# Block ends of a fused scan and expert kernel: the sixth product's bank summed later, and a last step with an order of its own

## The chip, the cores and the metric

One core of one Trainium2 chip. The metric is device microseconds of one execution. A ratio is the mean time of one kernel's fast runs over that of the other's in the same rounds, so it isn't quite the ratio of the medians that are quoted with it. "Span" is what the profile shows, from the first to the last instruction; the time of an execution is about 1.8 us longer.

## The reference

A Mamba-2 scan in chunks gives the rows of `x`, and four experts work on every row, weighted by probabilities:

```python
# x, B, C: (4, 8, 768, 32 or 16); out: (3072, 256)
x = attn_out.transpose(0, 2, 1, 3).reshape(3072, 256)
p = domain_probs / (domain_probs.sum(-1, keepdims=True) + 1e-09)
for e in range(4):
    h = np.maximum(x @ w1[e], 0.0)
    out += p[:, e:e + 1] * (h @ w2[e])
```

## The kernel before

All is fp32. The rows are worked in six blocks of 512. A block has eight steps, one for each pair of expert and slice of its hidden width. In a step both matrix products are done in seven products instead of eight (a Strassen-like scheme): `fmul` gives the first layer into banks X and Y, VectorE sums and gates them (`total`, `gated`) and takes differences T1 to T4 (`diff`), and `smul` adds the second layer's products to four PSUM banks `acc0` to `acc3`, two products a bank. The products of step n - 1 are issued between those of step n, so a block's last products fall into the next block's first step. There `keep` copies two banks to SBUF, and `combine` adds the products up to the result.

```python
ORDER = (1, 3, 7, 5, 6, 2, 4)            # products, two a bank: 6 and 2 share acc2

def combine(k, part, eng):
    p1, p3 = kept[k, 0][:, 0], kept[k, 0][:, 1]
    # ... o, u: result and partial sums in SBUF; b1, b2: halves of the block
    if part == 0:
        nc.vector.tensor_add(u[:, 0], acc[k, 2][:, 0], p1)      # product 6's half of acc2
    if part == 1:
        p7, p5 = kept[k, 1][:, 0], kept[k, 1][:, 1]
        eng.tensor_add(u[:, 1], u[:, 0], p7)
        eng.tensor_add(u[:, 2], u[:, 0], p5)
        eng.tensor_add(o[:, 1, b2], u[:, 1], p5)
        eng.tensor_add(o[:, 0, b2], u[:, 2], p3)
    if part == 2:
        nc.vector.tensor_add(o[:, 0, b1], acc[k, 2][:, 1], p1)
        nc.vector.tensor_add(o[:, 1, b1], acc[k, 3][:, 0], u[:, 1])

def leave(k, lo, n, queues):             # 32x32 transposes on VectorE, then 8 transfers
    # ...
    nc.vector.transpose(ot.rearrange("p d b j -> p d (b j)"), o[:, :, lo:lo + n])
    for q in range(P // 32):
        for d in range(2):
            queues[d].dma_start(out=dst[q, d], in_=ot[32 * q:32 * q + 32, d])

for n in range(NS + 1):                  # the last turn only finishes step NS - 1
    # ... products 1, 3, 7, 5 of step n - 1 between those of step n
    smul(n - 1, 6)
    if ending:                           # first step of a block
        combine(k - 1, 0, nc.vector)
        combine(k - 1, 1, nc.gpsimd if run else nc.vector)
        if not run:
            leave(k - 1, HB, HB, (nc.sync, nc.scalar))
    if run:
        diff(n, "T3", "22", "12")
    smul(n - 1, 2)
    if c_in is not None:
        scores(...); masked(...)         # the scan of the next block
    smul(n - 1, 4)
    if run:
        diff(n, "T1", "12", "11"); diff(n, "T2", "22", "T1"); diff(n, "T4", "21", "T2")
    if ending:
        combine(k - 1, 2, nc.vector)
        if not run:
            leave(k - 1, 0, HB, (nc.sync, nc.scalar))
```

Of the kernel before, what the change touches and what calls it, by code (L numbers as in the profile page):

```python
# [8 lines left out]
FP32 = mybir.dt.float32  # L9
# [3 lines left out]
P = 128  # L13
# [4 lines left out]
def kernel(  # L18
# [32 lines left out]
    nc = tc.nc  # L51
# [60 lines left out]
    def load_w1(n):  # L112
        e, jj = divmod(n % SPB, JJ)
        t1 = wt1[n] = wts.tile([P, 7, HB], FP32, tag="wt1", name="wt1")
        if n >= SPB:
            nc.sync.dma_start(out=t1, in_=w1_d[n % SPB])
            return
        for k in range(2):
            nc.sync.dma_start(
                out=t1[:, 2 * k:2 * k + 2],  # L120
                in_=w1[e, k * P:k * P + P].rearrange("p (a f) -> p a f", a=2)[
                    :, :, jj * HB:jj * HB + HB])

    def load_w2(n):
        e, jj = divmod(n % SPB, JJ)
        t2 = wt2[n] = wts.tile([P, 7 * HB], FP32, tag="wt2", name="wt2", bufs=4)
        if n >= SPB:
            nc.sync.dma_start(out=t2, in_=w2_d[n % SPB])
            return
        for i in range(2):  # L130
            f = i * FH + jj * HB
            nc.sync.dma_start(
                out=t2[:, i * 2 * HB:(i + 1) * 2 * HB].rearrange("p (j m) -> p j m", j=JJ),
                in_=w2[e, f:f + HB].rearrange("(j p) m -> p j m", p=P))
# [88 lines left out]
    def load_gate(k, e):  # L223
        g = gate[k, e] = ffn.tile([P, CPB, P], FP32, tag="gate", name="gate", bufs=3)
        nc.sync.dma_start(out=g, in_=p_d[CPB * k:CPB * k + CPB, e].partition_broadcast(P))
# [112 lines left out]
    def sums(k):  # L338

        y = yT[k]  # L340
        b1, b2 = slice(0, HB), slice(HB, BLK)
        Y = yS[k] = ffn.tile([P, 4, HB], FP32, tag="yS", name="yS")
        nc.vector.tensor_sub(Y[:, 0], y[:, 0, b2], y[:, 0, b1])
        nc.vector.tensor_sub(Y[:, 1], y[:, 1, b2], Y[:, 0])
        nc.vector.tensor_sub(Y[:, 2], y[:, 1, b2], y[:, 0, b2])
        nc.vector.tensor_sub(Y[:, 3], y[:, 1, b1], Y[:, 1])
# [4 lines left out]
    def fmul(n, i):  # L351

        k = n // SPB
        f = first.setdefault(n, {})
        bank = "X" if i in (1, 6, 7, 4) else "Y"
        if i in (1, 2, 5):
            f[bank] = ps_f.tile([P, JJ, HB], FP32, tag=bank, name=bank)
        y, Y = yT[k], yS.get(k)
        w = (A11, A12, S4, A22, S1, S2, S3)[i - 1]
        b1, b2 = slice(0, HB), slice(HB, BLK)  # L360
        rhs = {1: y[:, 0, b1], 2: y[:, 1, b1], 3: y[:, 1, b2]}.get(i)
        if rhs is None:
            rhs = Y[:, {4: 3, 5: 0, 6: 1, 7: 2}[i]]
        for j in range(JJ):
            nc.tensor.matmul(  # L365
                out=f[bank][:, j], lhsT=wt1[n][:, w, j * P:j * P + P], rhs=rhs,
                start=(i in (1, 2, 5) and j == 0), stop=(j == JJ - 1), skip_group_check=True)

    def snap(n, i):

        s = first[n][i] = ffn.tile([P, JJ, HB], FP32, tag="snap", name="snap", bufs=4)
        nc.scalar.copy(out=s, in_=first[n]["X"])  # L372

    def total(n, i, b):

        z = first[n]["z" + b] = ffn.tile([P, JJ, HB], FP32, tag="z", name="z", bufs=3)
        nc.vector.tensor_add(z, first[n]["Y"], first[n][i])  # L377

    def gated(n, b, src):

        if n not in hid:
            hid[n] = {}
        h = hid[n][b] = ffn.tile([P, JJ, HB], FP32, tag="h" + b, name="h" + b)
        k, e = n // SPB, n % SPB // JJ
        half = int(b[1]) - 1
        g = gate[k, e].rearrange("p c s -> p (c s)")[:, half * HB:half * HB + HB]
        nc.vector.scalar_tensor_tensor(  # L387
            out=h, in0=first[n][src], scalar=0.0, in1=g.unsqueeze(1).to_broadcast([P, JJ, HB]),
            op0=ALU.max, op1=ALU.mult)

    def diff(n, o, x, y):
        h = hid[n]
        h[o] = ffn.tile([P, JJ, HB], FP32, tag="h" + o, name="h" + o)
        nc.vector.tensor_sub(h[o], h[x], h[y])  # L394
# [22 lines left out]
        e = kept[k, u] = ffn.tile([P, 2, HB], FP32, tag=f"kept{u}", name=f"kept{u}", bufs=1)  # L417
        nc.scalar.copy(out=e, in_=acc[k, u])

    def combine(k, part, eng):  # L420

        p1, p3 = kept[k, 0][:, 0], kept[k, 0][:, 1]
        if part == 0:
            kept[k, "o"] = ffn.tile([P, 2, BLK], FP32, tag="o", name="o", bufs=1)
            kept[k, "u"] = ffn.tile([P, 3, HB], FP32, tag="u", name="u", bufs=1)
        o, u = kept[k, "o"], kept[k, "u"]
        b1, b2 = slice(0, HB), slice(HB, BLK)
        if part == 0:
            nc.vector.tensor_add(u[:, 0], acc[k, 2][:, 0], p1)  # L429
        if part == 1:  # L430
            p7, p5 = kept[k, 1][:, 0], kept[k, 1][:, 1]
            eng.tensor_add(u[:, 1], u[:, 0], p7)
            eng.tensor_add(u[:, 2], u[:, 0], p5)
            eng.tensor_add(o[:, 1, b2], u[:, 1], p5)
            eng.tensor_add(o[:, 0, b2], u[:, 2], p3)
        if part == 2:
            nc.vector.tensor_add(o[:, 0, b1], acc[k, 2][:, 1], p1)
            nc.vector.tensor_add(o[:, 1, b1], acc[k, 3][:, 0], u[:, 1])

    def leave(k, lo, n, queues):  # L440

# [10 lines left out]
    def opened(n):  # L452

        fmul(n, 1)
        snap(n, 1)
        fmul(n, 2)
# [38 lines left out]


    both = nc.sync, nc.sync
    for n in range(NS + 1):
        k, r = divmod(n, SPB)

        enter, exit = ({1: 0, 2: 1, 4: 2, 6: 3}, {2: 0, 3: 1, 5: 2, 7: 3}) if k == 0 else (
            {0: 0, 2: 1, 4: 2, 6: 3}, {1: 0, 3: 1, 5: 2, 7: 3})
        c_in, c_out = (CPB * (k + 1) + d[r] if r in d and k < NBLK - 1 else None
                       for d in (enter, exit))
        ending = r == 0 and k > 0
        run = n < NS
        if run:
            e = r // JJ
            if r % JJ == 0 and n + JJ < NS:
                load_gate(*divmod(n // JJ + 1, E))  # L510
            if n + 2 < NS:
                load_w1(n + 2)
                load_w2(n + 2)
            if n:
                opened(n)
                total(n, 1, "11")
                gated(n, "11", "z11")
        if c_in is not None:
            masks(c_in)
            decays(c_in)  # L520
        if n + 2 < NS:
            sum_w1(n + 2)
            sum_w2(n + 2)
        if r == 1 and k > 0:
            leave(k - 1, 0, BLK, both)
        smul(n - 1, 1)
        if run:
            if n == 0:
                fmul(n, 5)
            fmul(n, 6)  # L530
            snap(n, 6)
        smul(n - 1, 3)
        if ending:
            keep(k - 1, 0)
        if c_out is not None:
            outputs(c_out, ps_att, "att")
            added(c_out, ps_att, "att")
        if run:
            if n:
                fmul(n, 5)  # L540
            fmul(n, 7)
            snap(n, 7)
            total(n, 7, "22")
        smul(n - 1, 7)
        smul(n - 1, 5)
        if ending:
            keep(k - 1, 1)
        if run:
            gated(n, "22", "z22")
        if c_out is not None:  # L550
            carry(c_out)
            if c_out + 2 < NCH:
                load_chunk(c_out + 2)
        if run:
            fmul(n, 3)
            total(n, 6, "12")
            fmul(n, 4)
            gated(n, "21", "X")
            gated(n, "12", "z12")
            if r == SPB - 1 and k < NBLK - 1:  # L560
                sums(k + 1)
        smul(n - 1, 6)
        if ending:
            combine(k - 1, 0, nc.vector)
            combine(k - 1, 1, nc.gpsimd if run else nc.vector)
            if not run:
                leave(k - 1, HB, HB, (nc.sync, nc.scalar))
        if run:
            diff(n, "T3", "22", "12")
        smul(n - 1, 2)  # L570
        if c_in is not None:
            scores(c_in, ((ps_att, "att"), (ps_att, "att"), (ps_f, "X"), (ps_f, "Y")))
            masked(c_in, (2, 3, 0, 1))
        smul(n - 1, 4)
        if run:
            diff(n, "T1", "12", "11")
            diff(n, "T2", "22", "T1")
            diff(n, "T4", "21", "T2")
        if ending:
            combine(k - 1, 2, nc.vector)  # L580
            if not run:
                leave(k - 1, 0, HB, (nc.sync, nc.scalar))


# [43 lines left out]
```

## Time and profile before

| | |
|---|---|
| time, median of the four executions compared with the change | 680.52 us (679.91 to 680.96) |
| span of the profiled execution | 677.0 us |
| TensorE busy, share of the chain that ended last | 95%, 89% |
| TensorE halts on u, inside the run and in the last step | 5 of 0.85 us, 1 of 0.59 us |
| one product, start to start | 0.865 us |

The prediction below shows the lines.

### The profile page before, as it was taken

Reading aid. Unit: us, or ns where it says so; the run is one execution under the profiler, and the core shown is the slowest. Engines: PE = TensorE matmul, PEld = TensorE weight load, DVE = VectorE, ACT = ScalarE, POOL = GpSimd, SP = SyncE. Lnnn points to the kernel's source line nnn. Section 1 sums busy time; section 2 is a strip of 40 time slices with the busy share of each in tenths; the row PEclk is TensorE's granted clock in tenths of the full one; section 3 lists DMA queues with packets and bytes.
Section 4 is the critical chain, followed back from the end, with each engine's and each line's share of the span. In section 5 each row is a group of like instructions: output and inputs, shape, how many; then the busy total and the mean of one; then the engine's idle time right before and its main releaser. Section 6 shows DMA issues by size and latency. Waiting matters only on the chain.

```text
span 677.0 us, 9047 instructions
## 1 busy us (share of the span) xinstructions
PE 643.3 (95%) x3465; PEld 538.6 (80%) x3465; DVE 504.7 (75%) x821; ACT 116.2 (17%) x231; POOL 107.9 (16%) x153
## 2 busy tenths in 40 slices
PE   3779999999999999999999999999999999999995
PEld 1458788888888887888887888887888888888884
DVE  6979887697776867876878768668868776856655
ACT  1111112121211121121112111212211112111110
POOL 2976845001000002000002000002000000200000
PEclk9989999999999999999999999999999999999999
DMA  8997859636745554765364655554673543653202
GB/s 247 337 326 251 293 194 345 245 120 183 253 160 182 189 201 129 243 234 180 121 231 153 205 188 193 196 179 163 186 258 127 180 161 109 171 218 119 99 1 31
DMA packets 70938, 128.64 MB, mean 190 GB/s; under 512 B 29040, under 2 KB 52464, under 8 KB 70896
## 3 DMA queue, kind: packets, MB, share of 16 engines
q1 hardware_dynamic: 65688, 112.67, 49.3%
q0 software_dynamic: 2304, 14.68, 5.7%
q10 hardware_dynamic: 2904, 0.72, 0.5%
q8 instruction: 27, 0.44, 0.3%
q14 instruction: 15, 0.12, 0.1%
HBM read 109.99 MB, written 18.07 MB: 189 GB/s over the span
## 4 chain that ended last, share of the span: by engine, by line
PE 89%; DVE 6%; issue 0%; ACT 0%; POOL 0%; DMA 0%; DVEq 0%
PE acc L409 41%; PE X L365 24%; PE Y L365 19%; DVE h L387 2%; PE y L310 2%; PE g L271 2%; PE y L303 1%; DVE hT L394 1%; DVE LT L237 1%; DVE z L377 0%; DVE u L429 0%; PE A L292 0%; ACT snap L372 0%; DVE MT L281 0%; DVE ot L445 0%
## 5 line engine op out<-in xcount | busy, mean ns | idle before, releaser
L377 DVE TENSOR_TENSOR z<-Y,snap 128x512 f32<-128x512 f32 x144 | 99.0, 688 | 131.6 <-ACT snap L372 109.3
L409 PE MATMUL acc<-hT,wt 128*128 128x256 f32 x768 | 191.2, 382 | 0.0
L372 ACT COPY snap<-X 128x512 f32<-128x512 f32 x144 | 84.3, 585 | 487.8 <-PE X L365 481.5
L409 PEld LDWEIGHTS acc<-hT,wt 128*128 128x128 f32 x768 | 144.3, 190 | 25.4 <-issue 6.6
L409 PE MATMUL acc<-h,wt 128*128 128x256 f32 x576 | 148.3, 380 | 4.9 <-DVE u L429 4.9
L365 PE MATMUL X<-yS,wt 128*128 128x256 f32 x576 | 149.0, 381 | 0.7 <-ACT snap L372 0.7
L409 PEld LDWEIGHTS acc<-h,wt 128*128 128x128 f32 x576 | 108.9, 190 | 21.8 <-DVE u L429 7.3
L365 PEld LDWEIGHTS X<-yS,wt 128*128 128x128 f32 x576 | 110.4, 192 | 16.4 <-ACT snap L372 1.1
L387 DVE SCALAR_TENSOR_TENSOR h<-z,gate 128x512 f32<-128x512 f32 x144 | 104.5, 726 | 3.3
L365 PE MATMUL Y<-yT,wt 128*128 128x256 f32 x384 | 100.6, 385 | 1.5 <-DVE z L377 1.4
L365 PEld LDWEIGHTS Y<-yT,wt 128*128 128x128 f32 x384 | 72.7, 192 | 13.7 <-DVE z L377 2.3
L394 DVE TENSOR_TENSOR hT<-h,hT 128x512 f32<-128x512 f32 x96 | 69.7, 726 | 3.3
L394 DVE TENSOR_TENSOR hT<-h,h 128x512 f32<-128x512 f32 x96 | 66.8, 719 | 1.3
L244 POOL TENSOR_TENSOR bdec<-xb,LT 128x128 f32<-128x128 f32 x20 | 8.3, 413 | 343.8 <-issue 181.9
L237 DVE TENSOR_TENSOR_SCAN LT<-ab,ident 128x1024 f32<-128x1024 f32 x24 | 55.4, 2310 | 0.4
L365 PE MATMUL Y<-yS,wt 128*128 128x256 f32 x192 | 52.5, 397 | 2.1 <-DVE z L377 1.1
L365 PE MATMUL X<-yT,wt 128*128 128x256 f32 x192 | 50.6, 387 | 2.3 <-DVE MT L281 1.5
L365 PEld LDWEIGHTS X<-yT,wt 128*128 128x128 f32 x192 | 36.6, 193 | 9.1 <-DVE MT L281 2.3
L365 PEld LDWEIGHTS Y<-yS,wt 128*128 128x128 f32 x192 | 35.2, 192 | 8.9 <-DVE z L377 1.5
L281 DVE TENSOR_TENSOR MT<-g,LT 128x256 f32<-128x256 f32 x96 | 33.9, 414 | 10.5 <-PE g L271 10.4
L387 DVE SCALAR_TENSOR_TENSOR h<-X,gate 128x512 f32<-128x512 f32 x48 | 33.0, 688 | 6.1 <-PE X L365 6.1
L271 PE MATMUL g<-ctm,xb 32*128 32x256 f32 x192 | 19.0, 461 | 8.3 <-ACT ctm L262 8.3
(66 smaller groups left out, 267.1 us busy)
## 6 DMA issues: line engine op xcount, KB each, us to landing
wt<-w_d SPq DMA_DIRECT2D x80, 896.0 KB, 4.4
w_d<-wt POOLq DMA_DIRECT2D x16, 896.0 KB, 6.5
ab<-acut_d SPq DMA_DIRECT2D x22, 512.0 KB, 8.2
wt<-in_w_dram SPq DMA_DIRECT2D x32, 256.0 KB, 4.2
xb<-in_xbc_dram SPq DMA_DIRECT2D x24, 320.0 KB, 6.5
gate<-p_d SPq DMA_DIRECT2D x24, 256.0 KB, 6.0
out_dram<-ot SPq DMA_DIRECT2D x40, 64.0 KB, 2.0
ah<-ac_d SPq DMA_DIRECT2D x19, 64.0 KB
```

Source lines behind the costliest of these rows:

```text
L237: nc.vector.tensor_tensor_scan(out=LT, data0=s["ab"], data1=ident.rearrange("p h s -> p (h s)"), initial=0.0, op0=ALU.mult, op1=ALU.add)
L244: nc.gpsimd.tensor_mul(bdec, s["xb"][:, OB:OB + HN].rearrange("p (h n) -> p h n", h=NH), s["LT"][:, :, P - 1:P].to_broadcast([P, NH, N]))
L271: nc.tensor.matmul(out=g.rearrange("p t s -> p (t s)"), lhsT=s["xb"][k, OBT:OBT + P], rhs=s["ctm"][k].rearrange("p t s -> p (t s)"), start ...
L281: nc.vector.tensor_mul(s["MT"][:, h], s["g"][q], s["LT"][:, h])
L303: nc.tensor.matmul(out=y.rearrange("p t s -> p (t s)"), lhsT=state["M"].rearrange("p q d -> p (q d)"), rhs=s["cts"].rearrange("p t s -> p ...
L310: nc.tensor.matmul(out=y[32 * q:32 * q + 32, t], lhsT=xb[:, h * D:h * D + D], rhs=MT[:, NT * q + t], start=(first and t == 0), stop=True, ...
L365: nc.tensor.matmul(out=f[bank][:, j], lhsT=wt1[n][:, w, j * P:j * P + P], rhs=rhs, start=(i in (1, 2, 5) and j == 0), stop=(j == JJ - 1), ...
L372: nc.scalar.copy(out=s, in_=first[n]["X"])
L377: nc.vector.tensor_add(z, first[n]["Y"], first[n][i])
L387: nc.vector.scalar_tensor_tensor(out=h, in0=first[n][src], scalar=0.0, in1=g.unsqueeze(1).to_broadcast([P, JJ, HB]), op0=ALU.max, op1=ALU. ...
L394: nc.vector.tensor_sub(h[o], h[x], h[y])
L409: nc.tensor.matmul(out=acc[k, u][:, half], lhsT=w2_op(n, w)[:, j], rhs=rhs[:, j], start=(n % SPB == 0 and half == 0 and j == 0), stop=(n % ...
```

## The change

It is meant to take TensorE's halts away: at a block end u is read only when product 2 has filled the other half of the bank, behind the next block's scores and masks; the last step gets an order of its own, to have the first half of the result out early. Its words also promise the result in half as many transfers.

```diff
-        if ending:
-            combine(k - 1, 0, nc.vector)
-            combine(k - 1, 1, nc.gpsimd if run else nc.vector)
-            if not run:
-                leave(k - 1, HB, HB, (nc.sync, nc.scalar))
...
         smul(n - 1, 2)
         if c_in is not None:
             scores(...)
             masked(c_in, (2, 3, 0, 1))
+        if ending:
+            combine(k - 1, 0)
+            combine(k - 1, 1)
         smul(n - 1, 4)
...
+    finish(NS - 1)
...
+    def finish(n):
+        for i in (6, 1, 3):
+            smul(n, i)
+        keep(k, 0)
+        p1, p3 = kept[k, 0][:, 0], kept[k, 0][:, 1]
+        add(u[:, 0], acc[k, 2][:, 0], p1)
+        add(u[:, 1], u[:, 0], p3)
+        smul(n, 7)
+        smul(n, 5)
+        p7, p5 = acc[k, 1][:, 0], acc[k, 1][:, 1]
+        add(u[:, 2], p7, u[:, 0])
+        add(o[:, 1, b2], p5, u[:, 2])
+        add(o[:, 0, b2], p5, u[:, 1])
+        leave(k, HB, HB, (nc.sync, nc.scalar))
+        smul(n, 2)
+        add(o[:, 0, b1], acc[k, 2][:, 1], p1)
+        smul(n, 4)
+        add(o[:, 1, b1], acc[k, 3][:, 0], u[:, 2])
+        leave(k, 0, HB, (nc.sync, nc.scalar))
```

(`combine` loses its argument for the engine, the loop ends at `NS`, and the tests of `run` fall away. `leave` is unchanged.)

More of the change, by code (lines that the diff above doesn't have):

```diff
@@ L418, in keep, with combine @@
         nc.scalar.copy(out=e, in_=acc[k, u])
-    def combine(k, part, eng):
+    def combine(k, part):
         p1, p3 = kept[k, 0][:, 0], kept[k, 0][:, 1]
@@ L431, in combine @@
             p7, p5 = kept[k, 1][:, 0], kept[k, 1][:, 1]
-            eng.tensor_add(u[:, 1], u[:, 0], p7)
-            eng.tensor_add(u[:, 2], u[:, 0], p5)
-            eng.tensor_add(o[:, 1, b2], u[:, 1], p5)
-            eng.tensor_add(o[:, 0, b2], u[:, 2], p3)
+            nc.gpsimd.tensor_add(u[:, 1], u[:, 0], p7)
+            nc.gpsimd.tensor_add(u[:, 2], u[:, 0], p5)
+            nc.gpsimd.tensor_add(o[:, 1, b2], u[:, 1], p5)
+            nc.gpsimd.tensor_add(o[:, 0, b2], u[:, 2], p3)
         if part == 2:
@@ L438, in combine @@
             nc.vector.tensor_add(o[:, 1, b1], acc[k, 3][:, 0], u[:, 1])
+    def finish(n):
+        k = n // SPB
+        add = nc.vector.tensor_add
+        b1, b2 = slice(0, HB), slice(HB, BLK)
+        o = kept[k, "o"] = ffn.tile([P, 2, BLK], FP32, tag="o", name="o", bufs=1)
+        u = ffn.tile([P, 3, HB], FP32, tag="u", name="u", bufs=1)
+        for i in (6, 1, 3):
[16 more added lines that the diff above has]
+        leave(k, 0, HB, (nc.sync, nc.scalar))
     def leave(k, lo, n, queues):
@@ L497 @@
     both = nc.sync, nc.sync
-    for n in range(NS + 1):
+    for n in range(NS):
         k, r = divmod(n, SPB)
@@ L505 @@
         ending = r == 0 and k > 0
-        run = n < NS
-        if run:
-            e = r // JJ
-            if r % JJ == 0 and n + JJ < NS:
-                load_gate(*divmod(n // JJ + 1, E))
-            if n + 2 < NS:
-                load_w1(n + 2)
-                load_w2(n + 2)
-            if n:
-                opened(n)
-                total(n, 1, "11")
-                gated(n, "11", "z11")
+        e = r // JJ
+        if r % JJ == 0 and n + JJ < NS:
+            load_gate(*divmod(n // JJ + 1, E))
+        if n + 2 < NS:
+            load_w1(n + 2)
+            load_w2(n + 2)
+        if n:
+            opened(n)
+            total(n, 1, "11")
+            gated(n, "11", "z11")
         if c_in is not None:
@@ L526 @@
         smul(n - 1, 1)
-        if run:
-            if n == 0:
-                fmul(n, 5)
-            fmul(n, 6)
-            snap(n, 6)
+        if n == 0:
+            fmul(n, 5)
+        fmul(n, 6)
+        snap(n, 6)
         smul(n - 1, 3)
@@ L537 @@
             added(c_out, ps_att, "att")
-        if run:
-            if n:
-                fmul(n, 5)
-            fmul(n, 7)
-            snap(n, 7)
-            total(n, 7, "22")
+        if n:
+            fmul(n, 5)
+        fmul(n, 7)
+        snap(n, 7)
+        total(n, 7, "22")
         smul(n - 1, 7)
@@ L547 @@
             keep(k - 1, 1)
-        if run:
-            gated(n, "22", "z22")
+        gated(n, "22", "z22")
         if c_out is not None:
@@ L553 @@
                 load_chunk(c_out + 2)
-        if run:
-            fmul(n, 3)
-            total(n, 6, "12")
-            fmul(n, 4)
-            gated(n, "21", "X")
-            gated(n, "12", "z12")
-            if r == SPB - 1 and k < NBLK - 1:
-                sums(k + 1)
-        smul(n - 1, 6)
-        if ending:
-            combine(k - 1, 0, nc.vector)
-            combine(k - 1, 1, nc.gpsimd if run else nc.vector)
-            if not run:
-                leave(k - 1, HB, HB, (nc.sync, nc.scalar))
-        if run:
-            diff(n, "T3", "22", "12")
+        fmul(n, 3)
+        total(n, 6, "12")
+        fmul(n, 4)
+        gated(n, "21", "X")
+        gated(n, "12", "z12")
+        if r == SPB - 1 and k < NBLK - 1:
+            sums(k + 1)
+        smul(n - 1, 6)
+        diff(n, "T3", "22", "12")
         smul(n - 1, 2)
@@ L573 @@
             masked(c_in, (2, 3, 0, 1))
+        if ending:
+            combine(k - 1, 0)
+            combine(k - 1, 1)
         smul(n - 1, 4)
-        if run:
-            diff(n, "T1", "12", "11")
-            diff(n, "T2", "22", "T1")
-            diff(n, "T4", "21", "T2")
+        diff(n, "T1", "12", "11")
+        diff(n, "T2", "22", "T1")
+        diff(n, "T4", "21", "T2")
         if ending:
-            combine(k - 1, 2, nc.vector)
-            if not run:
-                leave(k - 1, 0, HB, (nc.sync, nc.scalar))
+            combine(k - 1, 2)
+    finish(NS - 1)
 def kernel(x, a, B, C, moe_domain_probs, moe_w1, moe_w2):
```

## The prediction

> **What bounds the kernel now.** I read the page's busy shares first, then its chain of work that ended last, to know which engine sets the time.
>
> ```profile
> PE 643.3 (95%) x3465; PEld 538.6 (80%) x3465; DVE 504.7 (75%) x821; ACT 116.2 (17%) x231; POOL 107.9 (16%) x153
> ...
> PE 89%; DVE 6%; issue 0%; ACT 0%; POOL 0%; DMA 0%; DVEq 0%
> ```
>
> TensorE is busy for 95% of 677.0 us and makes up 89% of the chain, so time is won only where TensorE stands still, or after its last product. The view of waits, for TensorE alone, lists the halts. The line that the change is aimed at is the third longest:
>
> ```profile
> PE g L271 <- ACT ctm L262: 8.3, 4, 5.1
> PE A L292 <- POOL bdec L244: 6.0, 3, 4.2
> PE acc L409 <- DVE u L429: 4.9, 6, 0.9
> ```
>
> (Total us, times, longest.) Six halts are the five block ends inside the run and the last step. The first two rows lie in the start-up, which the change doesn't touch. Next the timeline of one block end and of an ordinary step with the same instructions, TensorE alone (start, length, what):
>
> ```profile
> 150.38 1.03 PE L409 MATMUL acc<-hT,wt 128*128 128x256 f32 x4
> 152.26 1.13 PE L409 MATMUL acc<-h,wt 128*128 128x256 f32 x4 [0.85 <-DVE u L429]
> 153.32 0.71 PE L271 MATMUL g<-ctm,xb 32*128 32x256 f32 x8
> 153.97 1.13 PE L409 MATMUL acc<-hT,wt 128*128 128x256 f32 x4
> 154.93 0.38 PE L365 MATMUL X<-yT,wt 128*128 128x256 f32 x1
> ```
>
> ```profile
> 177.83 1.03 PE L409 MATMUL acc<-hT,wt 128*128 128x256 f32 x4
> 178.69 1.03 PE L409 MATMUL acc<-h,wt 128*128 128x256 f32 x4
> 179.65 0.71 PE L271 MATMUL g<-ctm,xb 32*128 32x256 f32 x8
> 180.30 1.13 PE L409 MATMUL acc<-hT,wt 128*128 128x256 f32 x4
> 181.26 0.38 PE L365 MATMUL X<-yT,wt 128*128 128x256 f32 x1
> ```
>
> The rows are product 6, product 2, the scores, product 4 and the next step's first product. At the block end product 2 waits for VectorE's sum u, which VectorE reaches only after two gating operations. From product 6 to the next step it takes 154.93 - 150.38 = 4.55 us; in the ordinary step 181.26 - 177.83 = 3.43 us. A block end thus costs **1.12 us** extra, more than the 0.85 of the waits (ends of matmuls are modelled 0.17 late, and a restart costs 0.10). A product takes 0.865 us from start to start. The fifth block end, at 575 us, has no scores: product 6 starts at 574.95 and the next step at 578.65, 3.70 us where three products take 2.60, so 1.10 extra.
>
> Last, the tail:
>
> ```profile
> 663.26 1.89 PE L409 MATMUL acc<-h,wt 128*128 128x256 f32 x8
> 663.52 1.42 DVE L394 TENSOR_TENSOR hT<-h,hT 128x512 f32<-128x512 f32 x2
> 668.33 1.13 PE L409 MATMUL acc<-h,wt 128*128 128x256 f32 x4 [0.59 <-DVE u L429]
> 669.84 0.71 DVE L445 STREAM_TRANSPOSE ot<-o 128x512 f32<-128x512 f32 x1
> 670.58 3.85 SPq L450 DMA_DIRECT2D out_dram<-ot  x8
> 671.23 0.71 DVE L445 STREAM_TRANSPOSE ot<-o 128x512 f32<-128x512 f32 x1
> ```
>
> The last step's products start at 663.26, the first half is transposed by 670.55, and its transfers go out from 670.58. SyncE issues eight transfers in 3.85 us, one every 0.49 us, ScalarE another eight beside it. The fifth, the first of the second half, is issued at 672.46 (seen in the same timeline cut into shorter windows), 0.52 us after the second transpose ended at 671.94. So the second half waits for the issuing queue, not the queue for it: the end at 677.0 hangs on when the **first** transpose is done, plus 6.4 us.
>
> **What the Trainium skill says.** "PSUM — Partial Sum Buffer", section "PSUM bank collisions raise a hardware error", asks for PSUM to be guarded by bank and quadrant, not by address. The trace agrees with an ordering of that kind: u reads one half of bank acc2, product 2 writes the other half, and it waits 0.85 us. "SBUF — State Buffer", section "Who interferes with whom", says that a VectorE instruction with two SBUF inputs contends with a GpSimd instruction that reads SBUF, and that one with at most one SBUF input does not. The trace agrees: at the fifth block end the pair of differences T2, T4, beside GpSimd's sums, takes 2.23 us against 1.42 us in the tail, and GpSimd's own sums 1.17 against 0.72 us. "DMA: Bandwidth & Descriptors", section "Issuing engines are not separate DMA queues", says issuing on several engines saves only the sequencer's time; here that time, 0.49 us per issue, is what the second half waits for.
>
> **The change part by part.** The order of the built program shows these moves.
>
> *Five block ends.* Product 2 no longer waits: in the built order its VectorE wait is gone. The sum u moves behind difference T3 and, at four ends, behind the four masks. Gain to be had: 4 x 1.12 + 1.10 = 5.58 us.
>
> What it gives back: GpSimd's four sums start after u, and now fall on VectorE's T1, T2, T4, which read two SBUF tiles. Before, GpSimd ran at four ends beside an idle VectorE (1.31 us) and the masks, whose first input is PSUM, so without contention. Working the first end through: product 2 starts at 151.24, scores at 152.20, masks at 152.99 (0.79 behind the scores, as before), u at 154.33, T1 at 154.67. T1, T2 and T4 at the spacings of the fifth end before (1.25, 1.13, 1.03; about 1.1 each) end near 158.0, two combines 0.67, then the next step's first total, 0.69, ends near 159.4. TensorE wants bank Y, which this total reads, for product 5, at 160.46 before, so at 160.46 - 1.12 = 159.34. Before, the total ended at 158.85, 1.6 us ahead; now it lands about together with the need. I put 0.15 us a time on this, 4 x 0.15 = 0.6.
>
> At the fifth end, T3 starts at 576.35, u must wait for product 2 (575.81 to 576.68, plus 0.25) and starts at 577.0, T1 at 577.34, T4 ends near 580.7, the combines at 581.4, the total at 582.1. Product 5, at 582.97 before, is wanted at 581.87. Wait about 0.25 plus a restart: 0.3 us.
>
> So block ends: 5.58 - 0.6 - 0.3 = **4.7 us won**.
>
> *The last step.* Order before: 1, 3, 7, 5, 6, wait, 2, 4. Now 6, 1, 3, 7, 5, 2, 4. Product 6 needs T2, the first of the pair starting at 663.52, done at 664.21. TensorE is free at 663.26, so it now waits until about 664.27: **1.01 us, a new wait**, where the old one was 668.33 - 667.59 = 0.74. Products 6, 1, 3, 7, 5 then take 0.96 + 4 x 0.865 = 4.42 and end at 668.69. One copy of a bank by ScalarE is gone, but it was not last. VectorE's u[2], 0.23 later, at 668.92, two sums 0.335 apart, the transpose 0.45 behind the last: it starts at 668.92 + 2 x 0.335 + 0.45 = 670.04 against 669.84. That is **0.2 us lost**. Only three sums follow the wait instead of five, but the wait ends later by a product and the T2 halt. The second transpose starts near 671.4, still ahead of the fifth issue.
>
> *The transfers.* The words of the change say half as many. The built program has the same eight of 32x8x32 on SyncE and the same eight on ScalarE. I follow the program: nothing, 0 us.
>
> Sum: 680.82 - 4.7 + 0.2 = **676.3 us**.
>
> **The rivals.** (1) The wait comes back in full as another: VectorE, slowed by GpSimd, makes TensorE wait for bank Y in every block end. For it: the missing slack worked out above, and 2.23 against 1.42 us. Against it: the delay is bounded by some 0.4 us an end, because before the next hard meeting VectorE has 2.38 us idle. If T1 to T4 are slowed more than I took, 0.5 us an end goes: 5.58 - 2.5 - 0.2 = 2.9 won, 677.9. (2) No contention that counts: the whole 5.58 stays, and the tail costs 0.2: 675.4. If the tail also gains (T2 early enough, transfers halved after all, which at 0.49 us an issue would save near 2 us), 673.5. I see nothing in the program for the latter. (3) The transpose at the next step waits for GpSimd's last sum, near 159.4 now instead of 155.45, and blocks the in-order VectorE. It would stand at 160.06, so it passes; were it late, the 2.38 us idle behind it would swallow the delay: no time.
>
> **Range and chances.** The middle case is 676.3. Rival 1 gives 677.9, rival 2 675.4, and the kernel before spread over 679.91 to 680.96 by itself. I take 674.6 to 678.1. A 2% change would be 13.6 us; all halts of the block ends together are 5.6. Chances: faster 0.01, within 2% 0.985, slower 0.005.
>
> **What would show each step.** In the profile after: the row of TensorE's waits for u at L429 gone; product 6 to next step about 3.4 us at four block ends; T1, T2, T4 near 1.1 us each there, GpSimd's sums up to 1.17; small new TensorE waits of bank Y for the total of line 377, 0.1 to 0.4 us, at block ends; one new wait of about 0.85 to 1.0 us of acc for hT (L394) in the last step; the stretch from the first transfer's issue to the end still near 6.4 us with eight issues per queue. Wrong would be: a tail shorter by over 0.5 us, bank Y halts over 0.6 us, or a block end still costing 1 us more than the ordinary step.

## More of the kernel before

One place is needed besides, since an error hangs on it: VectorE's timeline at the fifth block end (start us, length us, engine, line, operation).

```profile
576.35 0.42 DVE L429 TENSOR_TENSOR u<-acc,kept 128x256 f32<-128x256 f32 x1
576.69 1.81 DVE L394 TENSOR_TENSOR hT<-h,h 128x512 f32<-128x512 f32 x2
578.53 2.23 DVE L394 TENSOR_TENSOR hT<-h,hT 128x512 f32<-128x512 f32 x2
```

Behind u come two pairs: T3 and T1, then T2 and T4, beside GpSimd's sums. T3, first behind u, starts at 576.69, and T1 at 577.28; the next starts at 578.53. So the first operation behind u runs at its usual pace, and the stretching starts with the second.

## The result, and the profile after

674.07 us median (673.56 to 675.01, four executions) against 680.52 us; ratio 0.9907, interval 0.989 to 0.9925. That is inside the 2% to which the prediction gave a chance of 0.985, and 0.5 us under its range. The span of the profiled execution is 673.2 us.

First the waits of TensorE alone after the change, the two longest and those that answer to the line of u (waited for, total us, times, longest):

```profile
PE g L271 <- ACT ctm L262: 8.3, 4, 5.1
PE A L292 <- POOL bdec L244: 6.4, 3, 4.5
PE Y L365 <- DVE z L377: 1.4, 1, 1.4
...
PE acc L409 <- DVE hT L394: 0.8, 1, 0.8
```

The halts on u are gone. The bank Y halts on the total of line 377 that I expected in their place aren't there: the one of 1.4 us is in the start. The halt on hT is new, and is the last step's. Next TensorE's timeline at the first block end (product 6, product 2, scores, product 4, next step):

```profile
151.89 1.03 PE L409 MATMUL acc<-hT,wt 128*128 128x256 f32 x4
152.75 1.03 PE L409 MATMUL acc<-h,wt 128*128 128x256 f32 x4
153.71 0.71 PE L271 MATMUL g<-ctm,xb 32*128 32x256 f32 x8
154.35 1.13 PE L409 MATMUL acc<-hT,wt 128*128 128x256 f32 x4
155.32 0.38 PE L365 MATMUL X<-yT,wt 128*128 128x256 f32 x1
```

155.32 - 151.89 = 3.43 us, the same as the ordinary step: the whole 1.12 us is won. What follows on VectorE and GpSimd, to the total and to product 5, which needs bank Y:

```profile
155.83 0.41 DVE L429 TENSOR_TENSOR u<-acc,kept 128x256 f32<-128x256 f32 x1
156.16 0.68 DVE L394 TENSOR_TENSOR hT<-h,h 128x512 f32<-128x512 f32 x1
156.88 2.23 DVE L394 TENSOR_TENSOR hT<-h,hT 128x512 f32<-128x512 f32 x2
157.39 1.17 POOL L433 TENSOR_TENSOR u<-u,kept 128x256 f32<-128x256 f32 x1
159.70 0.68 DVE L377 TENSOR_TENSOR z<-Y,snap 128x512 f32<-128x512 f32 x1
160.85 1.13 PE L365 MATMUL Y<-yS,wt 128*128 128x256 f32 x4
```

The predicted contention is there: T2 and T4 take 2.23 us as a pair and GpSimd's second sum 1.17. But T1 takes 0.72 us from start to start (156.16 to 156.88), not the 1.25 I used. The contention met GpSimd first: its first sum starts at 156.39, 0.23 us after T1, and takes 1.04 us where its uncontended sums take 0.72. The total ends at 160.38, 0.47 us ahead of product 5, and TensorE doesn't notice. The third and fourth ends look the same (0.46, 0.47). At the fifth the total ends 0.22 us ahead, and at the second only 0.06:

```profile
264.91 0.67 DVE L377 TENSOR_TENSOR z<-Y,snap 128x512 f32<-128x512 f32 x1
265.64 1.13 PE L365 MATMUL Y<-yS,wt 128*128 128x256 f32 x4
```

There two matmuls of the scan (`y<-cts,M`, at 159.63 at the first end) are absent, so TensorE wants bank Y about 0.4 us sooner. Even so it doesn't wait: the start of the product before to product 5 takes 1.66 us (263.98 to 265.64), against 1.65 in the kernel before.

The last step: product 6, the first transpose, the transfers' issues.

```profile
660.19 1.13 PE L409 MATMUL acc<-hT,wt 128*128 128x256 f32 x4 [0.85 <-DVE hT L394]
666.06 0.71 DVE L471 STREAM_TRANSPOSE ot<-o 128x512 f32<-128x512 f32 x1
666.80 3.85 SPq L476 DMA_DIRECT2D out_dram<-ot  x8
```

TensorE would have been free for product 6 at 659.18 (the product before starts at 658.31, and a product takes 0.865), so it halts for 1.01 us, as predicted. From 659.18 to the end it takes 673.2 - 659.18 = 14.02 us; before, from 663.26 to 677.0, 13.74. So the last step loses 0.28 us.

The two profiled spans differ by 3.8 us, the medians by 6.45. What separates them is the start: product 6 of the first block end starts at 150.38 us before and at 151.89 after, though nothing in the program up to there has changed. From that instruction to the end it takes 526.62 us before and 521.31 after, **5.31 us less**, which is 5.58 won at the block ends less 0.28, within 0.01. The rest of this document calls this stretch "the part after the start".

### The profile page after: what moved, and what is told of

Same layout as the page of the kernel before. It is cut to its first block, busy times and chain, and to the rows that moved or that the text cites. A ratio compares the mean times of both kernels' runs of the same rounds, so it can differ in the third digit from the quotient of the medians.

```text
span 673.2 us, 9043 instructions
## 1 busy us (share of the span) xinstructions
PE 645.1 (96%) x3465; PEld 540.8 (80%) x3465; DVE 504.5 (75%) x821; ACT 115.6 (17%) x230; POOL 110.6 (16%) x153
## 4 chain that ended last, share of the span: by engine, by line
PE 91%; DVE 3%; DMA 2%; POOL 1%; SPq 1%; issue 0%; ACT 0%; ACTq 0%; POOLq 0%; DVEq 0%
PE acc L409 42%; PE X L365 25%; PE Y L365 19%; PE y L310 2%; PE g L271 2%; PE y L303 1%; DVE h L387 1%; DMA a_sb<-in_a_dram 1%; DMA wt<-in_w_dram 1%; DVE hT L394 1%; DMA ac_d<-a_sb 1%; POOL wt L146 0%; DVE z L377 0%; PE A L292 0%; ACT snap L372 0%
## 5 line engine op out<-in xcount | busy, mean ns | idle before, releaser
L365 PE MATMUL X<-yS,wt 128*128 128x256 f32 x576 | 150.6, 385 | 0.7 <-ACT snap L372 0.7
L387 DVE SCALAR_TENSOR_TENSOR h<-z,gate 128x512 f32<-128x512 f32 x144 | 102.8, 714 | 3.3
```

The source lines that it names most:

```text
L365: nc.tensor.matmul(out=f[bank][:, j], lhsT=wt1[n][:, w, j * P:j * P + P], rhs=rhs, start=(i in (1, 2, 5) and j == 0), stop=(j == JJ - 1), ...
L387: nc.vector.scalar_tensor_tensor(out=h, in0=first[n][src], scalar=0.0, in1=g.unsqueeze(1).to_broadcast([P, JJ, HB]), op0=ALU.max, op1=ALU. ...
```

## The experiments

The part after the start, from each trace, and the times (median, and ratio to the kernel before on the same chip):

| kernel | part after the start, us | its first product 6, us | median us | ratio, interval |
|---|---|---|---|---|
| before | 526.62 | 150.38 | 680.52 | |
| before_again | 526.60 | 152.60 | 679.89 | 0.9999, 0.9986 to 1.0012 |
| ends_only | 521.01 | 151.69 | 674.50 | 0.9921, 0.9908 to 0.9934 |
| last_only | 526.92 | 150.28 | 680.35 | 1.001, 0.9997 to 1.0023 |
| after | 521.31 | 151.89 | 674.07 | 0.9907, 0.989 to 0.9925 |
| after_again | 521.34 | 150.86 | 674.10 | 0.9923, 0.991 to 0.9937 |
| order_136 | 520.25 | 151.15 | 673.57 | 0.9912, 0.9895 to 0.9928 |
| half_sends | 521.76 | 151.04 | 676.17 | 0.9945, 0.9929 to 0.9961 |
| both_tails | 520.62 | 151.38 | 673.52 | 0.9911, 0.9894 to 0.9928 |
| late_vector | 525.74 | 151.26 | 678.85 | 0.9995, 0.9978 to 1.0012 |
| late_no_pool | 521.91 | 151.29 | 675.39 | 0.9932, 0.9916 to 0.9948 |
| row_sends | 518.52 | 151.38 | 671.46 | 0.987, 0.9853 to 0.9886 |

Spans are rounded to 0.1 us here. In both kernels that were traced twice the part after the start agrees within 0.03 us. The start moves by more than 2 us and doesn't follow the kernel. So one trace tells a tenth of a microsecond where the times, even of five rounds, don't.

**before_again: the kernel before against itself.** No edit.

> The kernel before against itself, to see how much of the 6.4 us is the start. Theory A (the change is worth 5.3 us, block ends +5.6 and last step -0.3, and the rest is how long TensorE ran at half its clock in the first 60 us of the executions that happened to be timed): ratio 1.000, but executions fall in two groups about 1 to 1.5 us apart, the longer ones with the lower granted clock (0.986 against 0.993). Theory B (the change shortens something that I haven't seen): all executions near 680.5 with the same clock as those of the changed kernel.

Ratio 0.9999, and the executions range from 678.65 to 680.99 us, with granted clocks from 0.982 to 0.992. These six follow the clock: 678.65 and 678.84 at 0.992, 679.77 to 680.43 at 0.985, 680.99 at 0.982, so three groups and not two. In the eleven executions of the same rounds' before the three at 0.982 are the longest (681.02 to 681.73), but in between the order isn't strict. Where the start goes shows in a stretch of 5 us (PE busy, PEld, DVE, ACT, POOL, granted clock, DMA share, GB/s). First the kernel before as it was first profiled, then the same kernel again:

```profile
45.00:50.00 5.00, 3.89 (x18) 3.12 (x17) 4.90 (x6) 1.76 (x4) 3.29 (x4) 1.00 1.03 324
```

```profile
45.00:50.00 5.00, 4.22 (x11) 2.88 (x10) 3.88 (x7) 0.70 (x2) 1.84 (x3) 0.50 0.68 230
```

In the second, TensorE was still at half its clock between 45 and 50 us and did 11 matmuls there, against 18. "TensorE: Matmul & The Clock Gate" of the Trainium skill, section "Part 1: The HAM clock gate (the "warmup" mystery)", calls the cold stretch run-variable, because the window that decides it runs free of the kernel; in this stretch the clock of one kernel was 1.00 in one execution and 0.50 in the other. Over the twelve traces the start goes with the mean granted clock, from 150.28 to 150.86 us at 0.993 to 152.60 at 0.982. That the clock accounts for all of that spread isn't shown: waits for GpSimd in the start differ too (6.0 us before, 7.2 us here, for line 292).

**ends_only: the block ends without the last step.**

```diff
-        if ending:
+        if ending and not run:
             combine(k - 1, 0, nc.vector)
-            combine(k - 1, 1, nc.gpsimd if run else nc.vector)
-            if not run:
-                leave(...)
+            combine(k - 1, 1, nc.vector)
+            leave(...)
...
+        if ending and run:
+            combine(k - 1, 0, nc.vector); combine(k - 1, 1, nc.gpsimd)
         smul(n - 1, 4)
```

> Only the block ends are changed, the last step stays as before. Theory A: product 6 to the next step takes 3.43 us at four ends and 2.6 at the fifth, 5.6 us less than before in sum; time about 5.6 us below before at the same granted clock. My prediction's sizes would give 4.7. Theory B (the last step is what gained): under 4.5.

The part after the start is 5.61 us shorter than before (526.62 - 521.01), and TensorE has no wait at all between 130 and 640 us. The block ends are worth all of their 5.58 us.

**last_only: the last step without the block ends.** `combine` of parts 0 and 1 goes back behind product 6; `finish` stays.

> Only the last step is changed, the block ends stay as before. Theory A: 0.2 to 0.3 us longer than before, a new TensorE wait of about 0.85 for T2 at the last step's start; span from the last product of the step before to the end 14.0 against 13.7 us. Theory B: 1 us shorter or more.

The part after the start is 0.30 us longer than before, with the new 0.8 us halt for hT. The ratio, 1.001, agrees without proving it. The two parts add up: -5.61 + 0.30 = -5.31, the change itself.

**after_again: the changed kernel again.** No edit.

> The changed kernel again. Theory A: 5.3 us below before where both have the same granted clock, ratio near 0.992; the ratio 0.9907 of the first comparison had more of its before executions in the longer group. Theory B: ratio 0.9907 again whatever the clocks.

Ratio 0.9923 against before, beside 0.9907 the first time; the first interval holds both values, the second just misses 0.9907. 0.9923 of 680.0 us, the mean of before in these rounds, is 5.2 us less, as the traces say.

**order_136: product 6 third.**

```diff
-        for i in (6, 1, 3):
+        for i in (1, 3):
             smul(n, i)
         keep(k, 0)
+        smul(n, 6)
```

> The changed kernel with its last step in the order 1, 3, 6, 7, 5, 2, 4, so that T2 is ready when product 6 needs it. If the wait for T2 is on the path: no wait of acc for hT in the last step, and from the last product of the step before to the first transpose 5.8 us against 6.9, so 1.1 us shorter than the changed kernel, ratio to before near 0.9905. If the tail hangs on something else (the queue of transfers): no shorter.

The halt for hT is gone and the part after the start is 1.06 us shorter than the changed kernel's. The last step's first products in TensorE's timeline, and the first transpose and the issues behind them:

```profile
658.44 1.89 PE L409 MATMUL acc<-h,wt 128*128 128x256 f32 x8
...
664.21 0.71 DVE L472 STREAM_TRANSPOSE ot<-o 128x512 f32<-128x512 f32 x1
...
664.95 3.85 SPq L477 DMA_DIRECT2D out_dram<-ot  x8
```

From 658.44 to the transpose 5.77 us, where the change has 666.06 - 659.18 = 6.88. The order that the change chose puts the product first whose operand is made last but one.

**half_sends: really half as many transfers, on the changed kernel; both_tails: the same on order_136.**

```diff
+        if k == NBLK - 1:
+            dst = out[r:r + n].rearrange("(b i) (d a j) -> a i d b j", i=32, j=32, d=2)
+            for q in range(P // 32):
+                queues[q % 2].dma_start(out=dst[q], in_=ot[32 * q:32 * q + 32])
+            return
```

> The changed kernel with the last block's result in really half as many transfers, four a queue instead of eight, each with both halves of the columns. If an issue costs 0.49 us whatever it carries: two issues done before the second half is transposed, the tail from the first issue to the end 0.5 us shorter (then bound by the transfers' own rate, 130 GB/s at 85% busy before) up to 1.4 us shorter. If an issue costs by its descriptors: about 0.98 us each and nothing won.

> Order 1, 3, 6, 7, 5, 2, 4 and half as many transfers together. The two lie one after the other on the path (first transpose, then transfers), so the gains should add: 1.1 + 0.5 = 1.6 us below the changed kernel if both work, 1.1 if only the order does.

Both expectations of a gain miss: the part after the start is 0.45 us longer than the changed kernel's, and with the better order 0.37 us longer than order_136. SyncE's issues in half_sends:

```profile
665.95 2.97 SPq L477 DMA_DIRECT2D out_dram<-ot  x4
```

Four issues take 2.97 us, 0.74 each against 0.49 each, and the last one ends 0.88 us sooner; still the end comes 6.85 us after the first issue and not 6.4. So, other than I had said, the tail doesn't hang on the issuing queue. In stretches of half a microsecond the data start about 0.3 us later after the first issue and then need about 3.9 us, as before. The traced execution of half_sends is its fastest, 674.58 us; the median, 676.17, lies further above the changed kernel's than the 0.45 us of the trace, and why stays open.

**late_vector: how much slack VectorE has at a block end.**

```diff
             combine(k - 1, 1)
+            diff(n, "T1", "12", "11")
         smul(n - 1, 4)
```

> The changed kernel with VectorE's T1 computed twice at each of the five block ends, to measure how much slack VectorE has there. In the changed kernel's trace the total of line 377 ends 0.47 us ahead of product 5's need at four ends, 0.2 at the fifth. One more operation beside GpSimd's sums makes it about 1.15 us later, so a halt of bank Y for the total of 0.65 to 0.8 us at four ends and 0.9 to 1.0 at the fifth, 3.5 to 4.2 us longer than the changed kernel in sum. If there is no slack, as I predicted: 1.2 a time, 6 us. If this chain isn't what TensorE meets next: no longer at all.

The part after the start is 4.43 us longer than the changed kernel's. VectorE at the first block end, with TensorE's answer (u, T1 twice, T2 and T4, the total, product 5):

```profile
155.20 0.41 DVE L429 TENSOR_TENSOR u<-acc,kept 128x256 f32<-128x256 f32 x1
155.53 1.81 DVE L394 TENSOR_TENSOR hT<-h,h 128x512 f32<-128x512 f32 x2
157.38 2.24 DVE L394 TENSOR_TENSOR hT<-h,hT 128x512 f32<-128x512 f32 x2
160.21 0.68 DVE L377 TENSOR_TENSOR z<-Y,snap 128x512 f32<-128x512 f32 x1
160.94 1.13 PE L365 MATMUL Y<-yS,wt 128*128 128x256 f32 x4 [0.65 <-DVE z L377]
```

From u to the total it is 5.01 us, 1.14 more than the 3.87 of the changed kernel, and product 5 halts 0.65 us. At the other ends the halts are 1.08, 0.65, 0.66 and 0.80 us; the expectation had overlooked how little the second end has to spare. So the chain that I feared is the right one. It starts to cost when VectorE is about 0.5 us later than the change makes it at three ends and about 0.2 us later at the fifth; at the second there is next to nothing left.

This run also tests whether place or operation decides, since T1 stands first and second behind u. Cut into shorter windows:

```profile
155.53 0.68 DVE L394 TENSOR_TENSOR hT<-h,h 128x512 f32<-128x512 f32 x1
156.13 1.22 DVE L394 TENSOR_TENSOR hT<-h,h 128x512 f32<-128x512 f32 x1
```

The same T1 takes 0.68 us in first place and 1.22 in second.

**late_no_pool: the same second T1, with three of GpSimd's four sums taken away.** Half of the first five blocks' results are wrong (relative error 0.84).

```diff
             nc.gpsimd.tensor_add(u[:, 1], u[:, 0], p7)
-            nc.gpsimd.tensor_add(u[:, 2], u[:, 0], p5)
-            nc.gpsimd.tensor_add(o[:, 1, b2], u[:, 1], p5)
-            nc.gpsimd.tensor_add(o[:, 0, b2], u[:, 2], p3)
+            nc.scalar.copy(out=o[:, 1, b2], in_=p5)
+            nc.scalar.copy(out=o[:, 0, b2], in_=p3)
```

> Late_vector again, T1 twice at every block end, but three of GpSimd's four sums there are replaced by copies on ScalarE of other data (half of the first five blocks' results wrong on purpose), so that T1, T2 and T4 run without GpSimd beside them. If GpSimd's reads are what stretches them: each 0.7 us, the total of line 377 no later than in the changed kernel, no halt of bank Y at the block ends, and the stretch from product 6 of the first block end to the end 521.3 us as in the changed kernel. If they are slow by themselves: halts of 0.65 us again and 525.7 us.

The part after the start is 3.83 us shorter than late_vector's and 0.6 us longer than the changed kernel's; one halt of 0.3 us remains, at the second end, where nothing was to spare, and product 5 of the fifth end comes 0.15 us late (578.76, against 577.75 + 0.865). The same place on VectorE:

```profile
155.57 1.81 DVE L394 TENSOR_TENSOR hT<-h,h 128x512 f32<-128x512 f32 x2
157.42 1.42 DVE L394 TENSOR_TENSOR hT<-h,hT 128x512 f32<-128x512 f32 x2
```

T2 and T4 take 1.42 us again, since GpSimd has only one sum left, and that one still stretches the second T1. So GpSimd's sums beside them are what stretches VectorE's differences; this run doesn't separate their reads from their writes.

**row_sends: order_136 with the last block's result in rows of 1 KB.** TensorE transposes 128x128 blocks into PSUM, ScalarE and VectorE copy them out, and four transfers carry whole rows.

```diff
-        leave(k, HB, HB, (nc.sync, nc.scalar))
...
-        leave(k, 0, HB, (nc.sync, nc.scalar))
+        rows(k, HB)
+        rows(k, 0)
+
+    def rows(k, lo):
+        for t, copy, queue in ((0, nc.scalar.copy, nc.sync), (1, nc.vector.tensor_copy, nc.scalar)):
+            s = slice(lo + t * P, lo + t * P + P)
+            pt = ps_att.tile([P, 2, P], FP32, tag="att", name="pt")
+            for d in range(2):
+                nc.tensor.transpose(pt[:, d], o[:, d, s], ident[:, 0])
+            # ... copy(out=row, in_=pt); queue.dma_start(out=out[rows of s], in_=row)
```

> Order_136 with the last block's result transposed by TensorE through PSUM, so that it leaves in four transfers of whole rows of 1 KB and not in sixteen of 128-byte pieces. If the tail hangs on the rate of the small pieces (4096 of them at 130 GB/s, 3.9 us): data transfer under 2 us, end about 1.3 us before order_136, 519.0 us from product 6 of the first block end to the end. If it hangs on the time from an issue to its landing: about as order_136, 520.2, or longer, since the transposes wait for product 4.

The part after the start is 518.52 us, 1.73 us less than order_136: the best version here, 671.46 us, ratio 0.987. From the last step's first product to the first issue it takes 0.35 us longer than in order_136 (665.53 - 658.67 = 6.86 against 664.95 - 658.44 = 6.51), yet the end comes sooner. The view of transfers over the last 15 us of this kernel:

```profile
DMA packets 576, 0.52 MB, mean 35 GB/s; under 512 B 64, under 2 KB 576, under 8 KB 576
```

576 packets move what took 4352 in the last 17 us of the kernel before, at up to 342 GB/s in a slice of this view, against about 130 GB/s there. That the pieces' size is what counts is shown only together with the other path through PSUM and the number of transfers, which changed with it; fewer transfers alone didn't help (half_sends).

## Why the prediction was wrong

- **Block ends, what is to be had (5.58 us): right.** Ends_only wins 5.61.
- **Block ends, what is given back (0.9 us): this step failed.** It ran: T1, T2 and T4 "at the spacings of the fifth end before (1.25, 1.13, 1.03; about 1.1 each) end near 158.0". The mechanism was right: T2 and T4 are stretched by GpSimd, and bank Y is what TensorE meets next, as late_vector and late_no_pool show. The term mis-sized is T1: 1.25 taken, 0.72 measured. At the fifth end before, T1 stood second behind u; after the change it stands first, where T3 had stood, and the first isn't stretched (0.59 from start to start for T3 there; T1 itself took 0.68 in first place and 1.22 in second in late_vector). This half microsecond is the whole difference between a total that lands with the need and one 0.47 us ahead. So 0.9 us of cost was none. The trace before had this clue too: at its first end T3, first behind u, took 0.68 us, and it was GpSimd's first sum beside it that took 1.04 against 0.72. The sum had taken four ends as alike: at the second the total did land with the need, 0.06 us ahead, and that it cost nothing there was luck. Rival 2's size (5.58 kept, the tail lost) came true, but not its reason: the contention is there.
- **The last step (0.2 us lost): right,** 0.28 in the trace, 0.30 in last_only; the halt of 1.01 us came as worked out.
- **The transfers, 0 us: right for the change,** which has the same sixteen. What I said they hang on was wrong: "the second half waits for the issuing queue, not the queue for it". Fewer issues made the tail longer (half_sends); larger pieces, on another path, made it shorter (row_sends). The 6.4 us from first issue to end did hold (666.80 to 673.2). The trace before had the clue: the data of the last block took about 4 us too, at about 130 GB/s with the DMA engines 85% busy, in 4352 packets under 512 bytes.
- **The start.** From 4.5 us predicted to 5.3 shown are 0.8 us; 680.82 - 5.3 = 675.5 would have been inside the range. So the failed step alone doesn't take the time out of the range. Another 0.3 us is that 680.82, the median of the three executions I had, became 680.52 with the fourth. The remaining 1.1 us or so, from 5.3 to 6.45, isn't the change's: the start moves by as much, and repeated it gave 0.9923. With 526.6, 521.3 and 1.8 us taken off, the mean start of the four executions before comes to 152.1 us and of the four after to 151.1 (an inference, since those weren't traced). I had read 679.91 to 680.96 as the spread of a kernel whose profiled execution took 678.77, and that execution alone should have told me that the spread is wider.

## What to carry to other kernels

When a wait is removed by moving an operation, take the durations of what is moved by the place in the queue behind its trigger, not by the operation's name: the first instruction behind a hand-over to another engine may run free where the second is stretched (0.68 and 1.22 us here for the same T1). Work out every place where the operation is moved to, since one of five alike had no time to spare. Order the last products by when their operands are ready, and look at the size of the pieces before counting transfers. Where the start of a kernel varies by more than the change is worth, measure from an instruction behind the start.

## What the Trainium skill lacked or had wrong

- "SBUF — State Buffer", section "Who interferes with whom": right on which instructions contend, but it has no duration for a two-input VectorE operation beside GpSimd's sums. Here 128x512 fp32 differences go from 0.71 to 1.12 us each, GpSimd's 128x256 sums from 0.72 to 1.17; one of each goes by in about 1.13 us, where one after the other would take 1.43.
- "DMA: Bandwidth & Descriptors", section "Issuing engines are not separate DMA queues", calls the time to initiate a transfer usually small beside the transfer. Here a queue's eight issues took 3.85 us and the data of both queues about 4 us. An issue of twice the pieces took 0.52 us inside the run (eight in 4.17) and 0.74 in half_sends, where it spans both halves of the columns, against 0.49; none of the pages cited has how an issue's time depends on its shape.
- "TensorE: Matmul & The Clock Gate", section "Part 1: The HAM clock gate (the "warmup" mystery)", puts the ramp's cost under 1% of a typical kernel. The start varied here by 2.3 us of 677, 0.3%, which doesn't contradict it (how much of this is the clock's isn't shown), and is still nearly half of what the change is worth.
